# Query weight means from ScalarE sums over the transposed tiles, without the natural copy, in a new order

## The chip, the cores and the metric

The kernel runs on one core of a Trainium2 chip. The metric is the device time of one execution in microseconds (us), lower is better. TensorE is written PE, VectorE DVE, ScalarE ACT, GpSimd POOL and SyncE SP, as in the profile. SP only issues DMAs; ACT issues two of its own at the start.

## The reference

One pre-norm transformer block on 2048 tokens of width 640, in bf16: linear attention with 32 heads of size 20 and a learned softmax feature map, then a gated product without activation.

```
def _A_ref(x, wqkv, w_phi, wo):
    qkv = (x @ wqkv).reshape(B, S, 3, H, Dh).transpose(2, 0, 3, 1, 4)
    q, k, v = qkv[0], qkv[1], qkv[2]
    pq = jnp.einsum("bhsd,hdf->bhsf", q, w_phi)
    pk = jnp.einsum("bhsd,hdf->bhsf", k, w_phi)
    phi_q = jnp.concatenate([_softmax(pq), _softmax(-pq)], axis=-1)
    phi_k = jnp.concatenate([_softmax(pk), _softmax(-pk)], axis=-1)
    kv = jnp.einsum("bhsf,bhsd->bhfd", phi_k, v)
    z  = jnp.einsum("bhsf->bhf", phi_k)
    num = jnp.einsum("bhqf,bhfd->bhqd", phi_q, kv)
    den = jnp.einsum("bhqf,bhf->bhq", phi_q, z)[..., None] + 1e-6
    return (num / den).transpose(0, 2, 1, 3).reshape(B, S, D) @ wo

h  = x + _A_ref(_layernorm(x), wqkv, w_phi, wo)
h2 = h + ((_layernorm(h) @ w_gate) * (_layernorm(h) @ w_up)) @ w_down
```

## The kernel before

The tokens are 16 tiles of 128. The mean that layernorm subtracts is taken out of the weights instead of the tokens: each column of the query, key and value weights loses its mean over the 640 inputs. For queries and keys the weights are also multiplied by the feature map in advance, so that one product per token tile gives the exponents. That needs the weights transposed: `WT[:, 0, a, :]` is the a-th of five transposed tiles of the query weights (written by a DMA transpose, `wqT`), `WT[:, 1, ...]` the same of the key weights (made by PE transposes of the natural copy `Wnat`). In the profile WT and Wnat both appear under the name phiqT, whose memory they share.

The small per-head matrices w_phi are loaded as `Wrows` (25 KB) by a DMA that ACT issues; five operations, three on DVE and two on POOL, spread them into `Phi`, the block-diagonal matrix with which every transposed weight tile is multiplied (the products `x0` to `x4` for the keys, `y0` to `y4` for the queries).

The start runs as follows. PE warms up on 38 products with ones, then for each of five rows of key weights takes five one-column products with ones (the means) and five transposes; ACT and DVE copy the first two transposed groups, DVE turns the means into `nmean` (line 775) and POOL spreads these into `nmuk` (line 777, tile outb); ACT (line 803) and DVE (line 806) subtract the mean from the other groups; then PE forms x0 to x4, with the statistics of the first tokens (`s0`, `s2`) and the column sums of the value weights (`wv`) between them. After that come keys `k`, values `v`, queries `q`, the sum over tokens `A`, the attention output `n`, the output weights `h`, and the gated product `f` and `D`.

The query means (`wq_means`) come a little later: 25 one-column products of the natural query weights with ones, a copy of the result to `nmeanq` (line 820), and five operations that add `nmeanq` to the transposed tiles (lines 829 and 832).

Every operation is recorded with its reads and writes and belongs to a named unit; the table `ORDER` says, for each of the five engines, in which order the units stand. Each engine's program is emitted in exactly that order, with semaphore waits where a value comes from another engine, so an instruction that waits holds everything behind it on its engine, the DMAs that this engine issues included. Where a unit has several operations on an engine, its name stands once for each. `place()` runs a model of times that decides how buffers are shared; a DMA recorded with `at=` counts there as landed at that time, wherever its engine issues it.

Of the kernel before, what the change touches and what calls it, by code (L numbers as in the profile page):

```python
# [7 lines left out]
ACT = mybir.ActivationFunctionType  # L8
# [39 lines left out]
WQ_POOL = ()  # L48

# [48 lines left out]
    "DVE":  # L98
# [16 lines left out]
    "ACT":  # L115
# [17 lines left out]
    "POOL":  # L133
# [300 lines left out]
def _build(ctx, nc, A_x, A_wqkv, A_w_phi, A_wo, B_w_gate, B_w_up, B_w_down, out):  # L434
# [5 lines left out]
    def regs(n):  # L440
        return [Reg() for _ in range(n)]
# [1058 lines left out]
```

## Time and profile before

| | us |
|---|---|
| median of 3 runs | 267.84 (267.67 to 268.1) |
| profiled execution, its own time | 267.55 |
| span of the profile, first to last instruction | 265.8 |
| PE busy | 260.4 (98%) |
| DVE busy | 222.7 (84%) |
| POOL busy | 190.1 (72%) |
| ACT busy | 177.2 (67%) |

The profiled execution is 0.29 us under the median, and 1.75 us of it lie outside the span. Busy is time in which an engine executes; matmuls overlap each other, so a row of them lasts a little longer than the distance to the next row. In rows of the timeline the columns are start, duration, engine, line, operation, output and inputs, shape, count, and in brackets the idle time before the row with what ended it.

### The profile page before, as it was taken

To read this page: it belongs to the slowest core of one execution; us is meant where nothing else is said; L and a number is where in the kernel's file an instruction comes from. 1 tells how busy PE (TensorE), PEld (TensorE's weight loads), DVE (VectorE), ACT (ScalarE), POOL (GpSimd) and SP (SyncE) were. 2 spreads that over 40 slices of the span, in tenths; PEclk is the share of its full clock that TensorE was granted. 3 is DMA by queue.
4 is the path that set the end of the run, shared out by engine and by line. 5 is a ranking of instruction groups with operands and counts; after the bars stand their busy time and mean duration, and the time that the engine had idled before them with its cause. 6 is when DMAs were issued, how large, how long until landed. Compare 5 with 4: busy or idle time off the path is not lost.

```text
span 265.8 us, 6243 instructions
## 1 busy us (share of the span) xinstructions
PE 260.4 (98%) x2418; PEld 200.0 (75%) x2433; DVE 222.7 (84%) x417; ACT 177.2 (67%) x387; POOL 190.1 (72%) x243
## 2 busy tenths in 40 slices
PE   8999999999999999999999999999999999999995
PEld 8877777776877787777767887777777777777773
DVE  1999999999999876998999778988778788675683
ACT  2567999999857998769553695764857555645220
POOL 5446989999932889999974789359866575648652
PEclk9999999999999999999999999999999999999999
DMA  7997999903155789666856515300410401001012
GB/s 188 302 138 175 165 233 401 382 32 75 39 82 100 89 247 210 130 106 133 131 115 128 47 25 79 99 4 0 56 45 19 83 0 52 1 2 51 14 65 71
DMA packets 67390, 28.65 MB, mean 108 GB/s; under 512 B 57632, under 2 KB 66080, under 8 KB 67360
## 3 DMA queue, kind: packets, MB, share of 16 engines
q1 hardware_dynamic: 66432, 27.90, 48.7%
q10 hardware_dynamic: 928, 0.35, 0.5%
q8 instruction: 19, 0.31, 0.5%
q14 instruction: 11, 0.09, 0.1%
HBM read 11.82 MB, written 2.62 MB: 54 GB/s over the span
## 4 chain that ended last, share of the span: by engine, by line
PE 85%; DVE 5%; DMA 3%; ACT 3%; issue 1%; POOL 1%; SPq 0%; ACTq 0%
PE ps L657 60%; PE ps L1210 24%; DMA phiqT<-eq 3%; ACT eq L933 1%; DVE ob L1075 1%; PE ps L746 1%; DVE x_all L1093 1%; DVE ps L925 1%; DVE Sq L987 1%; ACT phiqT L1335 0%; POOL eq L999 0%; DVE rden L1073 0%; DVE phiqT L806 0%; ACT junk L650 0%; ACT eq L1220 0%
## 5 line engine op out<-in xcount | busy, mean ns | idle before, releaser
L657 PE MATMUL ps<-Wp,xT 128*128 128x320 bf16 (+1 forms) x606 | 89.1, 299 | 0.0
L657 PEld LDWEIGHTS ps<-Wp,xT 128*128 128x128 bf16 x606 | 58.0, 98 | 22.5 <-ACT phik L933 0.3
L1240 POOL TENSOR_TENSOR phik<-phik,gate 128x512 bf16<-128x512 bf16 x34 | 40.1, 1184 | 25.9 <-DVE phik L1237 25.5
L1220 ACT ACTIVATE eq<-ps 128x256 f32<-128x256 f32 x110 | 37.4, 386 | 23.0 <-PE ps L1210 18.6
L1210 PE MATMUL ps<-phik,Wgu 128*128 128x256 bf16 (+1 forms) x214 | 46.6, 299 | 0.2
L950 POOL TENSOR_TENSOR phik<-phik,Rk 128x1280 bf16<-128x1280 bf16 x16 | 37.4, 2357 | 5.8 <-DVE Rk L949 4.8
L657 PE MATMUL ps<-phik,Wgu 128*128 128x256 bf16 (+1 forms) x259 | 33.2, 280 | 0.1
L657 PEld LDWEIGHTS ps<-phik,Wgu 128*128 128x128 bf16 x260 | 25.0, 98 | 5.5
L1337 POOL TENSOR_TENSOR phiqT<-phiqT,x_all 128x320 f32<-128x320 f32 x26 | 21.7, 844 | 9.7 <-ACT phiqT L1335 9.6
L925 DVE TENSOR_REDUCE ps<-ps 128x1 f32<-128x640 f32 (+1 forms) x32 | 26.1, 818 | 2.8 <-PE ps L657 2.8
L1210 PEld LDWEIGHTS ps<-phik,Wgu 128*128 128x128 bf16 x228 | 21.9, 98 | 5.7 <-ACT eq L1220 0.2
L657 PE MATMUL ps<-vaug,phik 128*128 128x63 bf16 (+1 forms) x308 | 25.9, 238 | 0.0
L987 DVE TENSOR_REDUCE Sq<-eq 128x66 f32<-128x1320 bf16 x16 | 24.2, 1513 | 1.4 <-ACT eq L933 1.4
L1237 DVE TENSOR_TENSOR phik<-ps,eq 128x512 bf16<-128x512 f32 x28 | 19.1, 687 | 6.3 <-PE ps L1210 6.2
L1335 ACT ACTIVATE phiqT<-ps 128x320 f32<-128x320 f32 x26 | 11.4, 437 | 19.3 <-PE ps L657 19.2
L947 DVE TENSOR_REDUCE Ssum<-phik 128x64 f32<-128x1280 bf16 x16 | 23.3, 1460 | 0.0
L1235 DVE TENSOR_TENSOR gate<-ps,eq 128x512 bf16<-128x512 f32 x27 | 18.5, 685 | 5.2 <-PE ps L1210 2.9
L657 PEld LDWEIGHTS ps<-vaug,phik 128*128 128x128 bf16 x308 | 18.1, 97 | 5.3
L999 POOL TENSOR_TENSOR eq<-eq,rq 128x660 bf16<-128x660 bf16 x16 | 20.9, 1305 | 0.8
L933 ACT ACTIVATE eq<-ps,nb,rs 128x300 bf16<-128x300 f32 (+2 forms) x26 | 17.2, 689 | 6.1 <-DVE nb L928 4.5
L1342 DVE TENSOR_TENSOR outb<-ps,phiqT 128x320 bf16<-128x320 f32 x28 | 13.4, 487 | 6.9 <-PE ps L657 5.5
L1139 ACT ACTIVATE gate<-ps 128x256 bf16<-128x256 f32 (+1 forms) x26 | 10.4, 406 | 10.3 <-PE ps L657 9.6
(168 smaller groups left out, 526.2 us busy)
## 6 DMA issues: line engine op xcount, KB each, us to landing
x_all<-in_A_x_dram SPq DMA_DIRECT2D x4, 640.0 KB, 10.7
out_dram<-outb SPq DMA_DIRECT2D x14, 160.0 KB, 1.9
Wgu<-in_B_w_gate_dram SPq DMA_DIRECT2D x1, 1920.0 KB, 10.6
Wgu<-in_B_w_up_dram SPq DMA_DIRECT2D x1, 1920.0 KB, 16.3
vaug<-in_B_w_down_dram SPq DMA_DIRECT2D x1, 1920.0 KB, 8.5
Wp<-in_A_wqkv_dram SPq DMA_DIRECT2D x1, 800.0 KB, 5.0
phiqT<-in_A_wqkv_dram SPq DMA_DIRECT2D x1, 800.0 KB, 6.4
Wo<-in_A_wo_dram SPq DMA_DIRECT2D x1, 800.0 KB, 6.0
```

The lines of the kernel that those rows point to most:

```text
L657: ins = e.matmul(o_, lhsT=l_, rhs=r_, start=s_, stop=p_, skip_group_check=True)
L925: g.op("DVE", lambda e: e.tensor_reduce(out=mx(), in_=src(), axis=AX.XY if len(src().shape) == 3 else AX.X, op=ALU.max, apply_absolute_val ...
L933: g.op("ACT", lambda e, s=s, sc=sc, to=to, of=of: e.activation(out=to(s), in_=of(), func=ACT.Exp, bias=nb[:, i:i + 1], scale=sc[:, t:t + 1 ...
L947: g.op("DVE", lambda e: e.tensor_reduce(out=Ssum[:, vs.i, :], in_=x, axis=AX.X, op=ALU.add), rd=R_phik[t], wr=vs.R, use=[vs], t=1.39, lat=1.5)
L950: g.op("POOL", lambda e: e.tensor_tensor(out=x, in0=x, in1=Rk[:, vr.i, :].unsqueeze(2).to_broadcast([P, 2 * H, DH]), op=ALU.mult), rd=vr.R ...
L987: g.op("DVE", lambda e: e.tensor_reduce(out=Sq[:, vs.i, :].rearrange("p (w g) -> p w g", w=NQ), in_=feat(0, NQ).rearrange("p w (g f) -> p ...
L999: return e.tensor_tensor(out=x, in0=x, in1=rq[:, vr.i, :].rearrange("p (w h) -> p w h", h=HW).unsqueeze(3).to_broadcast([P, NQ, HW, DH]), ...
L1210: ins = e.matmul(o_, lhsT=l_[0](c), rhs=m_, start=fr, stop=False, skip_group_check=True)
L1220: g.op("ACT", lambda e: e.activation(out=half(s[i], 256 * h, 256 * (h + 1)), in_=PS[v.i][:, bk, 256:512], func=ACT.Copy), rd=[v.R[bk]], wr ...
L1237: g.op("DVE", lambda e: e.tensor_tensor(out=hhT[:, hb_, ft, :], in0=PS[v.i][:, 1, :], in1=half(s[1]), op=ALU.add), rd=[v.R[1]] + s[1].R, w ...
L1240: g.op(eng, lambda e: e.tensor_tensor(out=hhT[:, hb_, ft, :], in0=hhT[:, hb_, ft, :], in1=gate[:, vg.i, :], op=ALU.mult), rd=R_out + vg.R, ...
L1337: g.op("POOL", lambda e: e.tensor_tensor(out=slot(x), in0=slot(x), in1=x_all[:, t, c], op=ALU.add), rd=x.R + [R_h[t]], wr=x.R, use=[x], t= ...
```

## The change

Five ACT sums over the transposed tiles (`wm0` to `wm4`, each with an accumulated row sum) give the query means, each in a register of its own; the 25 products with ones, the copy to `nmeanq` and the load of the natural query weights (`lwq`, 800 KB) are gone. The times that the planner's model assumes for loads and transposes are changed, and `ORDER` is written anew from start to end.

```
     def wq_means():
-        U("wm")
-        v = Buf(p_ps, 2)
-        g.op("PE", lambda e: mms(e, mean_mms(PS[v.i][:, 0, :], range(NC), 0)), rd=R_Wnat + [R_one], wr=v.R, use=[v], t=0.64, lat=0.79)
-        g.op("ACT", lambda e: e.activation(out=nmeanq[:, :], in_=PS[v.i][:, 0, 0:NC], func=ACT.Copy, scale=-1.0 / SC),
-             rd=[v.R[0]], wr=[R_nmu], use=[v], t=0.1, lat=0.23)
+        for a in range(NC):
+            U("wm%d" % a)
+            act_sum(WT[:, 0, a, :], ACT.Identity, nmeanq[:, a:a + 1], [R_WT[0][a]], [R_nmu[a]], scale=-1.0 / D)
...
-    U("lwq")
-    load_wnat(0)
     for a in range(NC):
         wqT(a)
...
     "ACT":
-        "in in in wk wk wk x2 x0 x4 k0 k0 k3 wm k1 k1 v2 v3 k3 k2 wq1 k2 v5 wq3 k7 v7 k7 k4 k4 v4 k6 k6 k5 v0 k5 s12 y4 y2 s12 y0 "
+        "in wk in wk wk in x2 x0 x4 wm4 wm2 k0 k0 k3 v3 k1 k1 k3 v2 wm3 k2 k2 wm0 wq3 v7 k7 k7 wm1 v5 wq1 v4 k6 k6 k4 k4 v0 k5 k5 "
```

Three places where instructions moved. First the start of ACT. Before (L549 is a DMA issue, L612 a one-element activation, L787 the copy of a transposed key group that waits for PE, L803 and L861 as above):

```order
L549 DMA phiqT<-in_A_wqkv_dram 128x2x640
L549 DMA Wrows<-in_A_w_phi_dram 128x5x20
L612 ACT_TABLE_LOAD
L612 ACTIVATE junk<-ones 128x1
L787 ACTIVATE phiqT<-ps 128x5x128
L803 ACTIVATE phiqT<-ps,nmean 128x384 x2
L861 ACTIVATE Wp<-ps 128x640 x3
```

The same place of ACT in the changed kernel, where the lines are L547, L610, L782, L794 and L846 and the new sums are L648:

```order
L547 DMA phiqT<-in_A_wqkv_dram 128x2x640
L782 ACT_TABLE_LOAD
L782 ACTIVATE phiqT<-ps 128x5x128
L547 DMA Wrows<-in_A_w_phi_dram 128x5x20
L794 ACTIVATE phiqT<-ps,nmean 128x384 x2
L610 ACTIVATE junk<-ones 128x1
L846 ACTIVATE Wp<-ps 128x640 x3
L648 ACTIVATE junk,nmeanq<-phiqT 128x640 x2
```

The DMA for Wrows now stands behind the copy that waits for PE, and two of the new sums stand behind the evacuations of x2, x0 and x4.

Second, the start of DVE, before (L784 is the copy of the first transposed key group, L636 spreads Wrows into Phi):

```order
L784 COPY phiqT<-ps 128x5x128
L636 TENSOR_TENSOR Phi<-Wrows,G 128x140 x2
L775 TENSOR_SCALAR nmean<-ps 128x5
L636 TENSOR_TENSOR Phi<-Wrows,G 128x160
L806 TENSOR_SCALAR phiqT<-ps,nmean 128x384 x3
```

The start of DVE in the changed kernel:

```order
L779 COPY phiqT<-ps 128x5x128
L634 TENSOR_TENSOR Phi<-Wrows,G 128x140 x2
L634 TENSOR_TENSOR Phi<-Wrows,G 128x160
L770 TENSOR_SCALAR nmean<-ps 128x5
L797 TENSOR_SCALAR phiqT<-ps,nmean 128x384 x3
```

The key means moved behind all three operations that read Wrows.

Third, PE from the last key product x4 on, before (Phi,phiqT is x4, xT with itself a token statistic, Wp,xT a projection, ones,phiqT the query means):

```order
L657 MATMUL ps<-xT 128x129 x5
L657 MATMUL ps<-Phi,phiqT 128x140 x2
L657 MATMUL ps<-Phi,phiqT 128x80 x2
L657 MATMUL ps<-Phi,phiqT 128x140 x2
L657 MATMUL ps<-xT 128x129 x5
L657 MATMUL ps<-Wp,xT 128x320 x30
L657 MATMUL ps<-ones,phiqT 128x1 x25
L657 MATMUL ps<-Wp,xT 128x320 x30
```

The same place of PE in the changed kernel:

```order
L655 MATMUL ps<-Phi,phiqT 128x140 x2
L655 MATMUL ps<-Phi,phiqT 128x80 x2
L655 MATMUL ps<-Phi,phiqT 128x140 x2
L655 MATMUL ps<-xT 128x129 x10
L655 MATMUL ps<-Wp,xT 128x320 x60
```

The 25 one-column products are gone from between the projections.

On SP the load lwq goes, the transposes of the query weights and of later token tiles follow the first four token tiles at once, and the loads of the gate and up weights move from ahead of the transposes of the first query features to between them.

More of the change, by code (lines that the diff above doesn't have):

```diff
@@ L47 @@
 CEN_POOL = ()
-WQ_POOL = ()
 NB = NT // 4
@@ L537, in _build @@
     R_Wo, R_Wgu, R_Wd = regs(NC), regs(2), Reg()
-    R_wsum, R_nmean, R_nmu, R_nmuk = regs(NC), regs(NC), Reg(), Reg()
+    R_wsum, R_nmean, R_nmu, R_nmuk = regs(NC), regs(NC), regs(NC), Reg()
     R_mv, R_sm, R_sxx, R_msq = regs(NT), regs(NT), regs(NT), regs(NT)
@@ L548, in load, with transpose @@
     def load(out_, in_, wr, mb, eng="SP", at=0.0):
-        return g.op(eng, lambda e: e.dma_start(out_, in_), wr=wr, dma=("w", 8), t=0.5, lat=0.4 if at else 1.9, size=mb / 0.38, at=at)
-    def transpose(out_, in_, rd, wr, use=(), t=1.27, size=1.07, lat=0.5, at=0.0):
+        return g.op(eng, lambda e: e.dma_start(out_, in_), wr=wr, dma=("w", 8), t=0.5, lat=0.4 if at else 0.6, size=mb / 0.38, at=at)
+    def transpose(out_, in_, rd, wr, use=(), t=1.27, size=0.45, lat=0.3, at=0.0):
         return g.op("SP", lambda e: e.dma_start_transpose(out_(), in_()), rd=rd, wr=wr, use=use, dma=("tr", 8), t=t, lat=lat,
@@ L587, in load_xT @@
     def load_xT(t, at=0.0):
-        transpose(lambda: xT[:, t, :, 0:P], lambda: A_x[0, P * t:P * (t + 1), :], [], [R_xT[t]], t=1.5, size=0.75, lat=1.25 if at else 2.75, at=at)
+        transpose(lambda: xT[:, t, :, 0:P], lambda: A_x[0, P * t:P * (t + 1), :], [], [R_xT[t]], t=1.5 if at else 1.4, size=0.75 if at else 0.62, lat=1.25 if at else 2.1, at=at)
     def load_x(b):
-        load(x_all[:, 4 * b:4 * b + 4, :], A_x[0, 4 * P * b:4 * P * (b + 1), :].rearrange("(t p) n -> p t n", p=P), [R_x[b]], 1.2)
+        load(x_all[:, 4 * b:4 * b + 4, :], A_x[0, 4 * P * b:4 * P * (b + 1), :].rearrange("(t p) n -> p t n", p=P), [R_x[b]], 0.9)
     def load_wv(c0, c1, at):
@@ L686, in f @@
                 return mms(e, lst)
-            g.op("PE", f, rd=[R_xT[t], R_one, R_xone], wr=[v.R[j // 2]], use=[v], t=0.125 if act else 0.282, lat=0.275 if act else 0.43)
+            g.op("PE", f, rd=[R_xT[t], R_one, R_xone], wr=[v.R[j // 2]], use=[v], t=0.19 if act else 0.282, lat=0.34 if act else 0.43)
             if act:
@@ L719, in stats @@
                 0.22, rd=R_sm[sl], wr=R_mv[sl])
-    def mean_mms(ps, cs, c0):
-        return [(ps[:, a:a + 1], Wnat[:, c, P * a:P * (a + 1)], ones[:, 0:1], a == 0 and c == c0, False) for c in cs for a in range(NC)]
     def wk_rounds():
@@ L797, in wk_rounds @@
             n = D - P * NRAW
-            if a in WQ_POOL:
-                pool_op(lambda e, a=a: e.tensor_scalar(out=WT[:, 0, a, :], in0=WT[:, 0, a, :], scalar1=nmeanq[:, a:a + 1], scalar2=None,
-                                                       op0=ALU.add), 1.0, rd=[R_nmu, R_WT[0][a]], wr=[R_WT[0][a]])
-                continue
             if a in (1, 3):
@@ L816, in wq_means @@
     def wq_means():
-        U("wm")
-        v = Buf(p_ps, 2)
-        g.op("PE", lambda e: mms(e, mean_mms(PS[v.i][:, 0, :], range(NC), 0)), rd=R_Wnat + [R_one], wr=v.R, use=[v], t=0.64, lat=0.79)
-        g.op("ACT", lambda e: e.activation(out=nmeanq[:, :], in_=PS[v.i][:, 0, 0:NC], func=ACT.Copy, scale=-1.0 / SC),
-             rd=[v.R[0]], wr=[R_nmu], use=[v], t=0.1, lat=0.23)
+        for a in range(NC):
+            U("wm%d" % a)
+            act_sum(WT[:, 0, a, :], ACT.Identity, nmeanq[:, a:a + 1], [R_WT[0][a]], [R_nmu[a]], scale=-1.0 / D)
         for a in range(NC):
             U("wq%d" % a)
-            if a in WQ_POOL:
-                pool_op(lambda e, a=a: e.tensor_scalar(out=WT[:, 0, a, :], in0=WT[:, 0, a, :], scalar1=nmeanq[:, a:a + 1], scalar2=None,
-                                                       op0=ALU.add), 1.0, rd=[R_nmu, R_WT[0][a]], wr=[R_WT[0][a]])
-                continue
             if a in (1, 3):
                 g.op("ACT", lambda e, a=a: e.activation(out=WT[:, 0, a, :], in_=WT[:, 0, a, :], func=ACT.Identity, bias=nmeanq[:, a:a + 1]),
-                     t=0.66, lat=0.8, rd=[R_nmu, R_WT[0][a]], wr=[R_WT[0][a]])
+                     t=0.66, lat=0.8, rd=[R_nmu[a], R_WT[0][a]], wr=[R_WT[0][a]])
                 continue
             g.op("DVE", lambda e, a=a: e.tensor_scalar(out=WT[:, 0, a, :], in0=WT[:, 0, a, :], scalar1=nmeanq[:, a:a + 1], scalar2=None,
-                                                       op0=ALU.add), t=0.3, lat=0.42, rd=[R_nmu, R_WT[0][a]], wr=[R_WT[0][a]], port=True)
+                                                       op0=ALU.add), t=0.3, lat=0.42, rd=[R_nmu[a], R_WT[0][a]], wr=[R_WT[0][a]], port=True)
     def wq_round(i):
@@ L1003, in queries @@
             SLOT_USERS.append(transpose(lambda w0=w0, w1=w1: phiqT[:, bb, w0:w1, P * tt:P * (tt + 1)], lambda w0=w0, w1=w1: eq[:, b.i, P * w0:P * w1],
-                      b.R + [R_pad], [R_phiqT[bb][k][tt]], [b], t=0.254 * (w1 - w0), size=0.214 * (w1 - w0)))
+                      b.R + [R_pad], [R_phiqT[bb][k][tt]], [b], t=1.3, size=0.5, lat=0.35))
     KVBUF = Buf(p_ps, 2)
@@ L1371, in wqT @@
         U("t%d" % a)
-        transpose(lambda: WT[:, 0, a, :], lambda: A_wqkv[:, P * a:P * (a + 1)], [], [R_WT[0][a]], t=1.5, size=0.75, lat=2.75)
+        transpose(lambda: WT[:, 0, a, :], lambda: A_wqkv[:, P * a:P * (a + 1)], [], [R_WT[0][a]], t=1.4, size=0.62, lat=2.1)
     U("warm")
@@ L1385, in _build @@
     U("lwo")
-    load(Wo[:, :, 0:D], A_wo.rearrange("(c p) n -> p c n", p=P), R_Wo, 1.5)
+    load(Wo[:, :, 0:D], A_wo.rearrange("(c p) n -> p c n", p=P), R_Wo, 0.95)
     for b in range(NB):
```

132 rows, old and new, of the table ORDER are left out of this document.

## The prediction

> **What bounds the kernel now.** I read the page's busy times first, then the busy time by stretches, then the timeline of the first 18 us engine by engine, since nearly all of the edit lies there.
>
> ```profile
> PE 260.4 (98%) x2418; PEld 200.0 (75%) x2433; DVE 222.7 (84%) x417; ACT 177.2 (67%) x387; POOL 190.1 (72%) x243
> ```
> ```profile
> 10.00:20.00 10.00, 10.00 (x116) 7.83 (x114) 9.85 (x22) 6.22 (x9) 4.55 (x13) 1.00 1.15 180
> 20.00:30.00 10.00, 10.00 (x88) 7.52 (x86) 9.60 (x25) 8.65 (x12) 7.25 (x9) 1.00 0.88 180
> ...
> 60.00:80.00 20.00, 19.71 (x303) 15.46 (x302) 19.26 (x39) 15.67 (x29) 15.51 (x12) 1.00 0.39 67
> 80.00:100.00 20.00, 19.90 (x205) 16.19 (x204) 17.12 (x30) 17.82 (x43) 13.07 (x23) 1.00 0.71 149
> 100.00:150.00 50.00, 49.73 (x448) 37.44 (x448) 44.72 (x85) 31.93 (x68) 42.22 (x56) 1.00 0.75 127
> 150.00:200.00 50.00, 49.63 (x408) 38.14 (x414) 41.20 (x76) 34.75 (x97) 37.34 (x48) 1.00 0.24 44
> ```
>
> After each stretch stand its length and the busy time of PE, weight loads, DVE, ACT and POOL, then the granted clock and the DMA share. From 10 us on PE is never idle for more than tenths: over 60 to 200 us it lacks 0.29 + 0.10 + 0.27 + 0.37 = 1.03 us. So from the moment that PE runs continuously, the end is that moment plus PE's work. Work taken from PE shortens the run; time that PE loses before its steady run is not caught up, save part of that 1.03 us. DVE is as full in 10 to 30 us (19.45 of 20), so it cannot help to catch up either. The question is when the steady run begins.
>
> ```profile
> 6.15 0.85 DVE L636 TENSOR_TENSOR Phi<-Wrows,G 128x140 bf16<-128x140 bf16 x2
> 7.36 0.17 DVE L775 TENSOR_SCALAR nmean<-ps 128x5 f32<-128x5 f32 x1 [0.36 <-PE ps L657]
> 7.44 0.32 DVE L636 TENSOR_TENSOR Phi<-Wrows,G 128x160 bf16<-128x160 bf16 x1
> 7.95 1.07 DVE L806 TENSOR_SCALAR phiqT<-ps,nmean 128x384 bf16<-128x384 bf16 x3 [0.19 <-PE ps L746]
> ```
> ```profile
> 7.46 0.44 PE L746 MATMUL ps<-ident,phiqT 128*128 128x128 bf16 x5
> 7.86 0.47 PE L657 MATMUL ps<-Phi,phiqT 128*128 128x140 bf16 x6
> 8.17 0.45 PE L657 MATMUL ps<-xT 128*128 128x129 bf16 x5
> 8.45 0.48 PE L657 MATMUL ps<-Phi,outb 128*128 128x140 bf16 x6
> 9.14 0.47 PE L657 MATMUL ps<-Phi,phiqT 128*128 128x140 bf16 x6 [0.21 <-DVE sm L698]
> ```
>
> The row at 7.86 is x1, the first user of Phi; it follows DVE's last Phi operation (7.44 + 0.32 = 7.76). The row at 9.14 is x3, which follows the last of the three subtractions on DVE (7.95 + 1.07 = 9.02). The steady run begins at 9.14.
>
> **The DMA of Wrows, moved behind a waiting copy.**
>
> ```profile
> 0.78 0.46 ACTq L549 DMA_DIRECT2D phiqT<-in_A_wqkv_dram  x1
> 1.28 0.49 ACTq L549 DMA_DIRECT2D Wrows<-in_A_w_phi_dram  x1
> ...
> 6.44 0.70 ACT L787 ACTIVATE phiqT<-ps 128x640 bf16<-128x640 bf16 x1 [3.15 <-PE ps L746]
> ```
> ```profile
> phiqT<-in_A_wqkv_dram ACTq DMA_DIRECT2D x1, 320.0 KB, 3.9
> ...
> Wrows<-in_A_w_phi_dram ACTq DMA_DIRECT2D x1, 25.0 KB, 4.6
> ```
> ```profile
> 5.98 0.86 POOL L636 TENSOR_TENSOR Phi<-Wrows,G 128x140 bf16<-128x140 bf16 x2 [1.93 <-DMA Wrows<-in_A_w_phi_dram]
> ```
>
> Before, the load is issued at 1.28, lands 4.6 us later at 5.88, and POOL, which had waited 1.93 us for it, starts at 5.98. Now it stands behind the copy that PE releases at 6.44. ACT works its list in order, so the issue comes at about 6.46, 5.2 us later than before. How long it then takes no row shows under these conditions. From below: the shortest load or store of the trace, 1.7 us. From above: 6.4 us, the 800 KB load issued at 7.94. Nearest are the same load's 4.6 us, which include the passage of 320 KB issued 0.5 us ahead on the same queue, and the 3.9 us of those 320 KB, which found ACT's queue empty, as the load does now. I take 3.9: landing at 10.4.
>
> ```profile
> out_dram<-outb SPq DMA_DIRECT2D x4, 80.0 KB, 1.7
> ...
> phiqT<-in_A_wqkv_dram SPq DMA_DIRECT2D x1, 800.0 KB, 6.4
> ```
>
> From the landing on the chain is forced by DVE's new order: 0.1 to the start (5.88 to 5.98 before), two Phi operations 0.85, the third 0.32, the means 0.17 with 0.05 to the next, three subtractions 1.07, and 0.12 to PE (9.02 to 9.14), in all 2.68. So x3 starts at 10.4 + 2.68 = 13.1 instead of 9.14: **+3.9 us**. The bounds 1.7 and 6.4 give +1.7 and +6.4. Behind the waiting Phi operations on DVE stand the key means, and with them POOL's nmuk, ACT's two subtractions, and behind x1 on PE everything else: nothing can be done ahead, and no later step has 3.9 us to give back.
>
> **The clock of PE.** While PE waits it stands still from about 7.7 (its transposes and the first statistic end there) to x1 at 10.4 + 0.1 + 0.85 + 0.32 + 0.1 = 11.8.
>
> ```profile
> 0.82 4.21 PE L657 MATMUL ps<-const-bfloat16-1.0 128*128 128x128 bf16 x38 [0.82 <-PEq L1485]
> ```
> ```profile
> 262.00:265.00 3.00, 0.88 (x7) 0.39 (x4) 1.08 (x3) 0.00 (x0) 0.00 (x0) 1.00 0.33 109
> 265.00:265.80 0.80, 0.00 (x0) 0.00 (x0) 0.00 (x0) 0.00 (x0) 0.00 (x0) 0.82 0.00 0
> ```
>
> At the start 38 products of 128 columns take 4.21 us, 111 ns each; the five transposes of 128 columns at 7.46 take 0.44 us with the way through the array in it, so PE then runs at about twice that rate. At the end PE falls still at 262.9 and the granted clock of the last 0.8 us is 0.82, so it has gone down within 2.9 us of the last product. A pause of 4.1 us is longer than that. So I expect PE to run its first products after the pause at half rate. What that costs is bounded by nothing (the short products x1 and x1's second part within the wait keep it up) and by half the stretch that was slow at the start, some 5 us from 0.82 on: 2.5 us. I take 1.0, two microseconds at half rate, nearer the lower end because about 0.9 us of products (the rows of 0.3 us distance at 7.86, 8.17 and 8.45) fall inside the wait and part of the slow time passes during it. The Trainium skill says the same in "TensorE: Matmul & The Clock Gate" (Part 1, the HAM clock gate): an idle window of about 3.4 us takes PE to 1.2 GHz, and a busy one brings it back; by it the loss would be up to 1.7 us for one window, and none if the free-running window falls badly for the gate.
>
> **The products removed.**
>
> ```profile
> 16.80 0.77 PE L657 MATMUL ps<-ones,phiqT 128*128 128x1 bf16 x25
> 17.43 4.24 PE L657 MATMUL ps<-Wp,xT 128*128 128x320 bf16 x30
> ```
>
> From the start of the 25 products to the next row are 0.63 us, all in PE's steady run: **-0.63**.
>
> **The sums added.** Each is one activation of 640 columns with a read of the accumulator, as in ACT's sums over Wo and x:
>
> ```profile
> 36.23 0.74 ACT L650 ACTIVATE junk<-x_all 128x640 bf16<-128x640 bf16 x1
> 36.85 0.20 ACT L650 ACTIVATION_READ_ACCUMULATOR junk<-x_all 128x1 f32 x1
> 36.95 1.30 ACT L861 ACTIVATE Wp<-ps 128x640 bf16<-128x640 f32 x2
> ```
> ```profile
> 15.50 0.88 ACT L933 ACTIVATE phik<-ps,nb,rs 128x640 bf16<-128x640 f32 x1 [2.19 <-DVE nb L928]
> ```
>
> From row to row 36.95 - 36.23 = 0.72 us, so five take 3.6 us. Two (1.44 us) stand where ACT idled 2.19 us for the first keys. Three (2.2 us) come in the next ten microseconds, where ACT has 1.35 us left (8.65 of 10), so about 0.8 us of ACT's work slides later; the copies and exponents there free score buffers for PE. The cover is the buffers that PE still has and the 3.8 us that ACT idles in 10 to 20; if it is gone PE waits for those 0.8 us. I cost it at nothing and keep 0.8 for the range.
>
> **The load removed and the rest of the new order.** lwq's 800 KB lie in saturated DMA time (share 1.15 in 10 to 20 us), but PE names no DMA as what it waits for after 9.14, so earlier transposes gain nothing. On SP the gate and up weights now follow transposes of the first query features, on POOL the order of small operations changes; what can be won by all this is the 1.03 us above, and a loss of the same size is as possible, since PE's spare time says how closely the orders fit. I take nothing, and ±1.0 for the range.
>
> **The sum.** 267.55 + 3.9 + 1.0 - 0.63 = 271.8 in terms of the profiled execution. The median is 0.29 above that execution, so 272.1.
>
> **The rivals.**
>
> *The load comes through quickly and PE keeps its clock.* For it: 25 KB are little, and a store of 80 KB needs only 1.7 us. Against it: the DMA share is over 1 around the new issue time, and the same 25 KB needed 4.6 us. With a landing 2.6 us after issue x3 starts at 11.7, +2.6, and without the clock term the time is 267.84 + 2.6 - 0.63 = 269.8; with 3.9 us and no clock term it is 271.1. The Trainium skill gives about 2.0 us fixed for one small DMA in "DMA: Bandwidth & Descriptors" (Anatomy of one DMA, measured there for GpSimd's path); by that the sum without the clock term would be 269.2, and the 4.6 us of this trace speak against it.
>
> *ACT becomes what PE waits for.* If the sliding work meets full score buffers, or the gate weights now hold up the query features behind them on SP, PE loses 0.8 to 2 us on top: 273 to 274. For it speaks that ACT is busy 17.82 of 20 us at 80 to 100; against it, that PE waits there for 0.10 us now.
>
> *The load isn't late: faster.* If ACT's list let a DMA pass the waiting copy, Wrows would land at 5.9 as before, and only the gains would stand: 267.84 - 0.63 = 267.2, and a little less, since DVE's third Phi operation now fills the 0.36 us for which DVE waits for the means. The point from which this decides is a landing before about 6.5, when DVE's chain is no later than now. Against it: no DMA row of ACT or SP in the timeline starts ahead of the row that its program puts before it.
>
> **How the numbers follow.** Late load with a clock drop, 270.9 to 273: 0.50. Late load, quick or without the drop, 269.2 to 270.9: 0.32. ACT or SP adds more, above 273: 0.10. Absorbed to within 0.2% (0.5 us, about what a measurement can tell from no change): 0.04. Not late: 0.04. The likeliest is 272.1; the range from 269.7 to 274.0 leaves out the fastest landings below, the worst pile-up above, and the two small cases. Faster 0.03, same 0.04, slower 0.93.
>
> **What would show it.** Right: ACT issues Wrows at about 6.5; POOL and DVE wait for its landing until 9 to 11; x1 starts near 11.8 and x3 near 13.1; the 25 one-column products are absent; the first key projections have twice their spacing for about two microseconds; from then on PE idles no more than before. Wrong: Wrows issued near 1.3 or landed before 8, x3 before 11, or PE stalls after 20 us that make up more than 1 us.

## The result, and the profile after

| | before | changed |
|---|---|---|
| median, us | 267.67 (267.04 to 268.1, 5 runs) | 276.46 (275.41 to 276.55, 5 runs) |
| profiled execution, its own time | 267.55 | 275.41 |
| span | 265.8 | 273.7 |

The ratio is 1.0322, with an interval of 1.0304 to 1.0340: 8.8 us slower, where 4.3 were forecast. The profiled execution is the fastest of the five, with a mean granted clock of 0.994; the other four had 0.988 and took 276.3 to 276.55 us.

The page's first line, and PE by stretches (columns as in the prediction):

```profile
PE 262.3 (96%) x2408; PEld 200.3 (73%) x2408; DVE 224.2 (82%) x417; ACT 180.5 (66%) x396; POOL 189.8 (69%) x243
```
```profile
12.00:14.00 2.00, 1.38 (x14) 1.41 (x15) 1.63 (x6) 1.15 (x3) 0.98 (x2) 0.54 0.71 129
14.00:16.00 2.00, 2.00 (x18) 1.64 (x16) 1.77 (x5) 0.00 (x0) 0.79 (x2) 0.61 0.74 139
```
```profile
30.00:40.00 10.00, 9.53 (x76) 6.52 (x74) 9.77 (x17) 9.87 (x16) 8.57 (x8) 1.00 0.89 213
...
80.00:100.00 20.00, 19.26 (x194) 15.19 (x195) 18.30 (x38) 15.30 (x34) 8.78 (x15) 1.00 0.74 125
...
150.00:200.00 50.00, 48.72 (x414) 37.10 (x412) 40.45 (x78) 31.33 (x87) 35.97 (x47) 1.00 0.32 53
```

The start, on ACT, DVE and PE:

```profile
6.24 0.70 ACT L782 ACTIVATE phiqT<-ps 128x640 bf16<-128x640 bf16 x1 [3.67 <-PE ps L741]
6.25 0.38 ACTq L547 DMA_DIRECT2D Wrows<-in_A_w_phi_dram  x1
```
```profile
11.24 1.20 DVE L634 TENSOR_TENSOR Phi<-Wrows,G 128x140 bf16<-128x140 bf16 x3 [5.12 <-DMA Wrows<-in_A_w_phi_dram]
```
```profile
12.62 0.76 PE L655 MATMUL ps<-Phi,phiqT 128*128 128x140 bf16 x6 [4.90 <-DVE nmean L770]
...
14.31 0.81 PE L655 MATMUL ps<-Phi,phiqT 128*128 128x140 bf16 x6
...
18.52 8.31 PE L655 MATMUL ps<-Wp,xT 128*128 128x320 bf16 x60
```

The load of Wrows is issued behind the copy, as forecast, and lands 5.0 us later. x3 starts at 14.31 instead of 9.14 (+5.17), the first key projections at 18.52 instead of 12.71 (+5.81): the further 0.64 us is the half clock, which the two windows show (2 x 0.46 + 2 x 0.39 = 1.70 us lost, so 3.4 us at half rate, of which about 0.5 us fall into PE's wait). With 0.63 us of products gone, 5.2 of the 7.9 us are explained at this point. The other 2.7 us come later, and the stretches show PE idle in three places where it was not before. I follow the last of them, around 150 us; that it counts for more than the other two is not shown.

There the seven-product stage begins: for the later token blocks `fu_seven` forms the gated products from seven half-size products, and ACT keeps halves of them (line 1220 before, 1205 now; "snapshots" below) in the memory of `eq`, where the exponents of the last queries stood until their DMA transposes into `phiqT` have read them. Before, on SP (the third of these transposes is issued at 144.53), ACT and PE:

```profile
141.93 3.89 SPq L553 DMA_TRANSPOSE phiqT<-eq  x3
```
```profile
148.97 0.38 ACT L1220 ACTIVATE eq<-ps 128x256 f32<-128x256 f32 x1 [2.21 <-DMA phiqT<-eq]
```
```profile
149.13 0.38 PE L1210 MATMUL ps<-Wp,phiqT 128*128 128x256 bf16 x2
149.41 0.39 PE L1210 MATMUL ps<-phiqT 128*128 128x256 bf16 x2
```

And after, where SP issues three such transposes in a row and the last one behind an output store:

```profile
148.04 3.92 SPq L551 DMA_TRANSPOSE phiqT<-eq  x3
152.01 0.58 SPq L1279 DMA_DIRECT2D out_dram<-outb  x1
152.63 1.22 SPq L551 DMA_TRANSPOSE phiqT<-eq  x1
```
```profile
157.06 0.66 ACT L1205 ACTIVATE eq<-ps 128x256 f32<-128x256 f32 x2 [3.59 <-DMA phiqT<-eq]
```
```profile
157.50 0.39 PE L1195 MATMUL ps<-phiqT 128*128 128x256 bf16 x2 [0.67 <-ACT eq L1205]
```

Before, the first snapshot ends at 149.35 and PE goes on at 149.41, 0.06 us later than its products follow each other anyway (0.22): the last transpose arrives just in time, with no slack. After, PE waits 0.67 us for the snapshot, a quarter of the 2.7 us. From the first snapshot to the end of the execution are 267.55 - 148.97 = 118.6 us before and 275.41 - 157.06 = 118.4 after. So the whole difference of the two executions is there when the first snapshot starts. The same holds for the experiments (profiled execution of each, us):

| kernel | last transpose issued | first snapshot | own time | own time less snapshot |
|---|---|---|---|---|
| before | 144.53 | 148.97 | 267.55 | 118.6 |
| before_stores | 145.97 | 150.24 | 268.79 | 118.6 |
| after_wrows | 146.51 | 149.39 | 268.05 | 118.7 |
| after_wrows_short | 146.74 | 151.40 | 269.76 | 118.4 |
| late_mid | 147.43 | 151.33 | 269.87 | 118.5 |
| late_stores | 146.97 | 150.99 | 269.36 | 118.4 |
| late_new | 147.51 | 151.74 | 270.13 | 118.4 |
| before_sums2 | 147.43 | 152.15 | 270.69 | 118.5 |
| after_wrows_pool | 148.28 | 152.55 | 270.44 | 117.9 |
| early_new | 148.22 | 152.59 | 271.15 | 118.6 |
| after_wrows_ones | 148.66 | 152.89 | 271.24 | 118.4 |
| before_sums | 148.94 | 153.53 | 272.06 | 118.5 |
| after_wrows_sp | 150.92 | 155.56 | 273.91 | 118.4 |
| before_late | 151.93 | 156.40 | 274.96 | 118.6 |
| after | 152.63 | 157.06 | 275.41 | 118.4 |
| after_warm | 154.49 | 157.38 | 275.83 | 118.5 |
| after_again | 155.62 | 159.88 | 278.23 | 118.4 |

The last column says where the time is lost, ahead of the snapshot, but not that the snapshot is the cause. Nearly the same work of PE stands behind the snapshot in every kernel, so the column would come out the same wherever ahead of it the time was lost; late_stores below is such a case.

### The profile page after: what moved, and what is told of

It reads as the page before. It is cut to its first block, busy times and chain, and to the rows that moved or that the text cites. A ratio compares the mean times of both kernels' runs of the same rounds, so it can differ in the third digit from the quotient of the medians.

```text
span 273.7 us, 6222 instructions
## 1 busy us (share of the span) xinstructions
PE 262.3 (96%) x2408; PEld 200.3 (73%) x2408; DVE 224.2 (82%) x417; ACT 180.5 (66%) x396; POOL 189.8 (69%) x243
## 4 chain that ended last, share of the span: by engine, by line
PE 70%; DMA 7%; POOL 6%; DVE 6%; ACT 5%; SPq 3%; issue 2%; ACTq 0%; DVEq 0%
PE ps L655 48%; PE ps L1195 22%; DMA phiqT<-eq 4%; SPq L551 3%; ACT eq L918 2%; DMA Wrows<-in_A_w_phi_dram 2%; POOL phik L935 2%; DVE Sq L972 1%; DMA phik<-ob 1%; POOL eq L984 1%; DVE phik L1133 1%; ACT junk L648 1%; POOL Wp L1149 1%; POOL rs L1098 1%; DVE ob L1060 1%
## 5 line engine op out<-in xcount | busy, mean ns | idle before, releaser
L1205 ACT ACTIVATE eq<-ps 128x256 f32<-128x256 f32 x112 | 38.2, 386 | 25.6 <-PE ps L1195 21.1
L1195 PE MATMUL ps<-phik,Wgu 128*128 128x256 bf16 (+1 forms) x228 | 51.0, 305 | 0.6 <-ACT t L1205 0.6
L655 PE MATMUL ps<-phik,Wgu 128*128 128x256 bf16 (+1 forms) x260 | 33.9, 281 | 0.1
L1220 DVE TENSOR_TENSOR gate<-ps,eq 128x512 bf16<-128x512 f32 x29 | 19.8, 686 | 7.8 <-PE ps L1195 3.1
L1222 DVE TENSOR_TENSOR phik<-ps,eq 128x512 bf16<-128x512 f32 x27 | 18.5, 686 | 5.9 <-PE ps L1195 5.9
L655 PE MATMUL ps<-Phi,phiqT 128*128 128x63 bf16 (+3 forms) x236 | 13.3, 203 | 6.1 <-DVE nmean L770 4.9
```

Of the source, the lines that this page charges most:

```text
L655: ins = e.matmul(o_, lhsT=l_, rhs=r_, start=s_, stop=p_, skip_group_check=True)
L1195: ins = e.matmul(o_, lhsT=l_[0](c), rhs=m_, start=fr, stop=False, skip_group_check=True)
L1205: g.op("ACT", lambda e: e.activation(out=half(s[i], 256 * h, 256 * (h + 1)), in_=PS[v.i][:, bk, 256:512], func=ACT.Copy), rd=[v.R[bk]], wr ...
L1220: g.op("DVE", lambda e: e.tensor_tensor(out=gate[:, vg.i, :], in0=PS[v.i][:, 0, :], in1=half(s[0]), op=ALU.add), rd=[v.R[0]] + s[0].R, wr= ...
```

## The experiments: the start

Ratios are to the kernel before, run on the same chip, with 95% intervals. In diffs of the order, the name ahead is the engine.

**after_wrows.** The late load undone.

```
ACT
- in wk in wk wk in x2 x0 x4 wm4
+ in in in wk wk wk x2 x0 x4 wm4
```

> The changed kernel with one thing undone: ScalarE again issues the load of Wrows before its first copy, as in the kernel before; the sums and the rest of the new order stay. Theory A (the loss has two parts: the late Wrows, which starts the first key projection 5.8 us later, 5.2 us of it wait and 0.6 us clock, and another 2 to 3 us of stalls further on that the sums or the new order make): 276.5 - 5.2 - 0.6 to 1.7 = 269.6 to 270.7 us, still slower than before, and the stall of TensorE near 35 to 37 us (about 1 us) is there 5 to 6 us earlier. Theory B (everything follows from the late Wrows): 267.7 - 0.6 = 267.0 us. The wait of VectorE for Wrows (5.12 us) is gone in both.

Median 270.47 us (268.05 to 271.69), ratio 1.0111 (1.0093 to 1.0130). Six us of the loss are the late load, 2.7 are not: theory A. The profiled execution is the fastest of its seven runs (five took 270.35 to 270.49), so its trace is not typical of the 2.7 us.

**before_late.** The late load alone, the opposite edit to the kernel before.

> The kernel before with one thing changed: ScalarE issues the load of Wrows behind its first copy, in the changed kernel's place; no sums, old order otherwise. Theory A (the late Wrows costs the same by itself): 267.7 + 5.2 + 0.6 to 1.7 = 273.5 to 274.6 us, Wrows landing near 11.2 us and a stretch of half clock between 10 and 16 us. Theory C (the load is slow in the changed kernel only because other loads were reordered around it): landing 3.9 us after its issue, as forecast, and 272 to 273 us. Theory D (the start is mostly absorbed later): under 271 us.

Median 273.88 us, ratio 1.0236 (1.0212 to 1.0259): 6.1 us, the same from the other side, so theory C and D fall. The landing was later than in the changed kernel's profile. The chain of waits (start, duration, what):

```profile
6.42 6.42 DMA Wrows<-in_A_w_phi_dram
```

**after_again.** The changed kernel a second time.

> The changed kernel unchanged, for a second profile of it: the first one was of its fastest execution (275.4 us, clock 0.994), while its other four took 276.3 to 276.6 us at a clock of 0.988. Theory A (in those, Wrows lands later than the 5.0 us of the first profile, by up to 1.5 us, and a second stretch of half clock falls into the start): landing near 6.4 us, half clock for 6.8 us. Theory B (the landing is the same, and the difference lies in the later stages): landing near 5.0 us.

Its profiled execution took 278.23 us (clock 0.988), 1.7 us more than the slowest of the first five; the other one took 275.76. Chain, PE and clock:

```profile
6.04 6.99 DMA Wrows<-in_A_w_phi_dram
```
```profile
14.43 0.76 PE L655 MATMUL ps<-Phi,phiqT 128*128 128x140 bf16 x6 [6.92 <-DVE nmean L770]
...
20.85 3.42 PE L655 MATMUL ps<-Wp,xT 128*128 128x320 bf16 x24
```
```profile
10.00:12.00 2.00, 0.00 (x0) 0.00 (x0) 0.00 (x0) 0.00 (x0) 0.00 (x0) 0.90 0.61 87
12.00:14.00 2.00, 0.00 (x0) 0.00 (x0) 0.95 (x3) 0.00 (x0) 0.90 (x2) 0.50 1.08 192
14.00:16.00 2.00, 1.57 (x16) 1.60 (x17) 1.62 (x7) 1.15 (x3) 0.79 (x2) 0.50 0.71 138
16.00:18.00 2.00, 2.00 (x15) 1.49 (x13) 1.76 (x5) 0.00 (x0) 0.79 (x2) 0.50 1.75 108
18.00:20.00 2.00, 2.00 (x27) 1.67 (x26) 1.01 (x4) 0.56 (x1) 1.44 (x5) 0.89 0.38 81
```

Theory A: the same load in the same place lands 5.0 us after its issue in one execution and 7.0 in another, and with the longer pause comes a second stretch of half clock (3.42 us of clock missing in these windows, 6.8 us at half rate; the part up to 14.43 falls into the pause itself).

**after_warm.** PE kept busy while it waits.

```
+        U("w2")
+        g.op("PE", lambda e: mms(e, [(PS[vx[1].i][:, 0, 0:P], one, one, True, True) for _ in range(80)]), ...
PE
- wk wk s0 x1 s0 x1 x3
+ wk wk s0 w2 x1 s0 x1 x3
```

> The changed kernel with 80 products of a 128-column constant put on TensorE between its first statistics and the first product that waits for Phi; they do no work for the result and end before the wait does (80 x 0.056 us = 4.5 us of the 4.9 us). Theory A (the wait costs a stretch of half clock as well as itself): the clock stays at 1.0 up to the end, and the time falls by the 0.6 us seen in the profiled execution up to the 1.7 us of one whole window, to 274.8 to 275.9 us. Theory B (the clock is no part of the loss): 276.5 us, or more if the products hold the first waiting product back.

Median 276.38 us (275.71 to 277.28), no different from 276.46: in the time, theory B. But the profile shows the clock kept up and the landing late:

```profile
6.32 6.56 DMA Wrows<-in_A_w_phi_dram
```
```profile
14.29 0.47 PE L655 MATMUL ps<-Phi,phiqT 128*128 128x140 bf16 x6 [1.80 <-DVE nmean L770]
...
19.08 5.19 PE L655 MATMUL ps<-Wp,xT 128*128 128x320 bf16 x37
```

From x1 to the first key projections are 19.08 - 14.29 = 4.79 us here, 18.52 - 12.62 = 5.90 with one stretch of half clock and 20.85 - 14.43 = 6.42 with two; before it was 12.71 - 7.86 = 4.85. So the clock costs 1.1 to 1.6 us at the start. That the medians don't show it I can't settle: the landing varies by more (1.6 us between these two profiles), and only profiled executions show it.

## The experiments: the sums and the new order

All kernels of this section have Wrows early.

**after_wrows_short.** The sums' time taken away.

```
- act_sum(WT[:, 0, a, :], ..., scale=-1.0 / D)
+ act_sum(WT[:, 0, a, 0:32], ..., scale=-1.0 / 32)
```

> The changed kernel with the early Wrows, and each of the five ScalarE sums taken over 32 of the 640 columns: order, waits and dependences stay, only the time of the sums falls, by about 5 x 0.5 us (the means are then rough ones). Theory A (ScalarE is the crowded engine between 13 and 41 us, and the sums' own time is what is left of the loss): 270.5 falls by 2 to 3.4 us, to 267 to 268.5 us. Theory B (the rest of the loss is the new order, not the sums): unchanged within 0.5 us, 270 to 271 us.

270.30 us, ratio 1.0106 (1.0090 to 1.0121): unchanged. In this order the sums' own time costs nothing that can be measured.

**after_wrows_ones.** The new order without the sums.

```
- act_sum units wm0 to wm4, R_nmu of five registers
+ U("lwq"); load_wnat(0); U("wm") with the 25 products and the copy
PE:  + wm behind k3 k1     SP: + lwq ahead of t4
DVE: - k3 wq2 k3 k1 k1 wq4     + k3 k3 wq2 k1 k1 wq4
```

> The changed kernel's order with the early Wrows, and without the sums: the natural query weights are loaded again, the 25 one-column products and one copy stand where the kernel before had them among the keys, and VectorE takes wq2 one step later. It is the new order alone against the kernel before. Theory A (the sums make what is left of the loss): 267.7 us, within 0.7. Theory B (the order makes it): 270 to 271.5 us, with TensorE's stalls between 80 and 170 us as in the changed kernel.

270.53 us, ratio 1.0109 (1.0090 to 1.0128). The new order alone costs as much as order and sums together: theory B. That the products with ones cost nothing against the sums does not follow, since the 800 KB load came back with them, and PE now waits 0.52 us at 36.45 us for a transposed token tile. late_new below is the cleaner test.

**after_wrows_sp.** SP back to the old order, the other engines not.

> The changed kernel with the early Wrows and, on SyncE alone, the order of the kernel before (less the load of the natural query weights); the sums and all other orders stay. Theory A (the sums on ScalarE): unchanged, 270.5 us or a little less, since two transposed query tiles come earlier. Theory B (SyncE's new order, which issues the query features' transposes elsewhere among its loads, makes the stalls between 80 and 170 us): 268 to 269.5 us.

273.22 us, ratio 1.0214 (1.0192 to 1.0236): worse, which neither theory had. The engines' orders fit each other, and exchanging one of them alone does not tell what it is worth.

**before_sums** and **before_sums2.** The sums in the old order.

```
ACT, before_sums
- x4 k0 k0 k3 wm k1 k1 v2 v3 k3 k2 wq1 k2 v5 wq3 k7 v7 k7
+ x4 wm4 k0 k0 k3 wm2 k1 k1 v2 v3 k3 wm3 k2 wq3 k2 v5 wm1 wq1 k7 v7 wm0 k7
ACT, before_sums2
+ x4 wm4 wm2 k0 k0 k3 k1 k1 v2 wm3 v3 k3 k2 wm1 k2 wq1 v5 wq3 k7 v7 k7 wm0
```

> The kernel before with the sums alone: the 25 one-column products and the load of the natural query weights are gone, the five ScalarE sums stand where ScalarE waited in the kernel before (behind x4, behind the first exponents of k3, and between k3 and k7), Wrows stays early, all other orders as before but for wq0, which VectorE takes two key tiles later. Theory A (ScalarE has room: it is idle 4.7 us between 13 and 41 us in the kernel before, and five sums of 0.67 us less the copy of 0.17 us need 3.2 us): 267.7 - 0.6 = 267.0 us. Theory B (the sums crowd ScalarE in that stage wherever they stand, and cost what stays unexplained in the changed kernel): 269 to 270 us.

271.55 us, ratio 1.0145 (1.0128 to 1.0162). PE waits for an exponent that stands behind a sum, and DVE for the last sum:

```profile
20.80 1.53 PE L657 MATMUL ps<-Wp,xT 128*128 128x320 bf16 x10 [0.68 <-ACT phik L931]
```
```profile
31.39 1.05 DVE L830 TENSOR_SCALAR phiqT<-phiqT,nmeanq 128x640 bf16<-128x640 bf16 x1 [1.44 <-ACT junk L650]
```

> The kernel before with the sums alone, placed better than in the first such kernel: two of them in ScalarE's wait of 2.2 us ahead of the first key exponents, one in its wait ahead of v3, the last two among the exponents of k2 and k7; VectorE takes wq0 three steps later, and SyncE issues the second transposed query tile right behind the first. Theory A (the sums take the place of the 25 products at no cost if nothing waits for them): 267.0 us (-0.6), up to no change, and the 3.8 us of the first such kernel was the places: ScalarE's sums of 0.7 us on the chain ahead of exponents and evictions, and VectorE's wait of 1.4 us for the last sum. Theory B (the sums cost ScalarE's room in any place): 268.5 to 271 us.

270.85 us, ratio 1.0113 (1.0093 to 1.0134): better placed by 0.7 us, still 3.05 us slower. PE loses more than half of it in the key stage, by stretches:

```profile
20.00:30.00 10.00, 8.87 (x76) 6.60 (x77) 8.84 (x22) 9.49 (x15) 6.40 (x8) 1.00 0.85 168
30.00:40.00 10.00, 9.45 (x99) 7.13 (x97) 9.63 (x24) 8.94 (x15) 8.14 (x8) 1.00 0.83 228
```

Here the sums do cost: PE idles 1.13 + 0.55 us in these stretches; before, by the row below and the one in the prediction, 0.06.

```profile
30.00:40.00 10.00, 9.94 (x110) 7.77 (x109) 9.97 (x24) 9.52 (x16) 8.95 (x10) 1.00 0.87 206
```

I found no place for them in the old order that doesn't; that there is none isn't shown.

**early_new** and **late_new.** Orders spliced on all engines at the end of the first attention products, near 75 us: the sums and the new order ahead of it and the old order behind, and the other way round without the sums.

> The changed kernel with the early Wrows, its sums and its new order up to the end of the first attention products (near 75 us), and from there on, on every engine, the order of the kernel before. Theory A (the rest of the loss, 2.7 us, lies in the new order of the later stages, where GpSimd stands 4 us before a sum and TensorE then waits twice for its weight sums): 267 to 268 us. Theory B (it lies in the new order of the key stage, where the first query product waits for the last sums): 269.5 to 270.5 us.

269.26 us, ratio 1.0055 (1.0035 to 1.0074), runs spread from 267.57 to 271.15. The profile is of the slowest run. It is on time up to the splice and beyond: an operation on DVE that starts at 85.44 us before starts at 85.44 here. The loss comes behind that, where both kernels have the same order. SP issues two transposes right behind the load of the down weights (w_down, 1920 KB), and they take 2.6 us longer; ACT waits 2.32 us for them, and PE for ACT. Before, on SP and PE:

```profile
94.10 5.76 SPq L553 DMA_TRANSPOSE phiqT<-eq  x2
```
```profile
105.25 0.51 PE L657 MATMUL ps<-Phi,phiqT 128*128 128x63 bf16 x11 [0.22 <-ACT eq L933]
```

In early_new:

```profile
93.60 8.35 SPq L548 DMA_TRANSPOSE phiqT<-eq  x2
```
```profile
107.33 0.51 PE L652 MATMUL ps<-Phi,phiqT 128*128 128x63 bf16 x11 [1.70 <-ACT eq L915]
```

Whether the early order brings such slow transposes about, or chance does, is not shown.

> The kernel before (products with ones, natural weights loaded, its own order) up to the end of the first attention products, and from there on, on every engine, the changed kernel's order. Theory A (the late part of the order makes the loss): 269.5 to 270.5 us, with TensorE's two stalls of 0.5 to 0.8 us near 162 and 171 us that follow GpSimd's wait. Theory B (the early part makes it): 267.3 to 268.2 us.

270.44 us, ratio 1.0102 (1.0080 to 1.0124). The late part alone has the whole loss. Nothing but `ORDER` differs from the kernel before here, so neither the sums nor the planner's changed times are needed for it. The early part alone has about half of the loss in the median, and the two don't add up (1.75 + 2.93 against 2.73 with both); why is not shown.

**after_wrows_pool.** GpSimd's weight sums ahead of its wait.

```
POOL
- T3 h8 h8 h11 h10 h9 G2.1 h8 h11 G2.3 T2 f1.1.0
+ T3 h8 h8 G2.1 G2.3 T2 h11 h10 h9 h8 h11 f1.1.0
```

> The changed kernel with the early Wrows and one more edit, on GpSimd alone: three sums of weights (G2.1, G2.3 and T2) stand ahead of the statistics of tile 11, for which GpSimd waited 4.0 us with the sums behind it. Theory A (this wait delays the weight sums, and TensorE's stalls near 162 and 171 us, 0.5 and 0.8 us, are its price): 269.0 to 269.5 us, those stalls gone. Theory B (TensorE would wait for something else there): 270.5 us.

270.56 us, ratio 1.0106 (1.0076 to 1.0136): theory B by the time. GpSimd's wait comes after the first snapshot and, without this edit, for a statistic of ACT that stands behind it, so it is late because that stage is late. In the profile the edit did part of what theory A says: after_wrows_short, with the same order but for this edit (and with shorter sums), has GpSimd waiting 4.00 us up to 152.95 us and PE 0.62 up to 161.45, and here both waits are gone. From the first snapshot to the end are 117.9 us, 0.5 to 0.8 less than in all other profiles. The interval of the ratio is too wide to show half a microsecond.

**late_mid.** The new order only from 75 us to the first product of the second block's feed-forward stage.

> The kernel before up to the end of the first attention products, the changed kernel's order from there to the first product of the second block's feed-forward stage, and the order of the kernel before again from there on. Theory A (the loss of the late order lies in the stage from 75 to 150 us, where transposes, projections and feed-forward products of one block are interleaved): 269.5 to 270.5 us, as with the whole late order. Theory B (it lies in the order of the seven-product stage from 150 us on): 267.3 to 268.2 us.

269.90 us, ratio 1.0086 (1.0066 to 1.0106): theory A for the greater part (2.1 of 2.9 us; the two intervals overlap, so that the rest lies in the later order is not shown). Most of the time is lost ahead of the seven-product stage, in when it can begin.

**before_stores.** The last transpose delayed, and nothing else.

```
SP
- Q15 n14 Q13 Q13 Q15 n12 ... h9 h10 d0 d1 D0.1
+ Q15 n14 Q13 Q13 d0 d1 Q15 n12 ... h9 h10 D0.1
```

> The kernel before with one edit on SyncE: the two stores of the first output tiles, which it issues some 10 us later otherwise, stand ahead of the last transpose of the query features (Q15's), which is issued at 144.53 us in the kernel before and for whose landing ScalarE waits 2.2 us with its first snapshot for the seven-product stage at 148.97 us. A store takes 0.58 us of issue. Theory A (the last query-feature transpose sets the start of the seven-product stage, so that whatever makes it later makes the end later by as much): last transpose and first snapshot 1.2 us later, time 268.5 to 269.0 us. Theory B (that stage has slack, and the kernels' losses lie elsewhere): 267.5 to 267.9 us.

268.50 us, ratio 1.0032 (1.0021 to 1.0044); the profiled execution 268.79, 1.24 us above that of before, its first snapshot 1.27 us later. SP, ACT and PE:

```profile
144.87 1.05 SPq L1294 DMA_DIRECT2D out_dram<-outb  x2
145.97 1.22 SPq L553 DMA_TRANSPOSE phiqT<-eq  x1
```
```profile
150.24 0.38 ACT L1220 ACTIVATE eq<-ps 128x256 f32<-128x256 f32 x1 [3.23 <-DMA phiqT<-eq]
```
```profile
149.39 0.38 PE L1210 MATMUL ps<-Wp,phiqT 128*128 128x256 bf16 x2
150.68 0.39 PE L1210 MATMUL ps<-phiqT 128*128 128x256 bf16 x2 [0.91 <-DVE phiqT L1164]
```

Theory A: the last transpose was the cause here. The operations of ACT and DVE stand in the same order in both kernels; just ahead of the snapshot they start 0.25 us later than before, and from 157 us to the end 1.27 us later. Two stores of half a microsecond of issue on SP thus cost the run 0.9 us in the median. (The row names a DVE operation that ends at the same moment as the snapshot; before, the same product at 149.41 starts ahead of that operation, which stands at 149.61, so it isn't what the product needs.)

**late_stores.** The store that the new order puts ahead of the last transpose, behind it.

```
SP
- Q15 Q15 Q13 d1 Q13 n12
+ Q15 Q15 Q13 Q13 d1 n12
```

> The kernel before with the changed kernel's order after the first attention products, and with one edit on SyncE: the store of an output tile, which there stands ahead of the last transpose of the query features, stands behind it. Theory A: last transpose and first snapshot 0.6 us earlier (147.5 and 151.7 us without the edit), time 269.8 us instead of 270.4. Theory B: 270.4 us, unchanged.

Last transpose 0.54 us earlier, first snapshot 0.75, the profiled execution 0.77 (269.36 against 270.13). But the two profiles differ ahead of the edit too, by up to 1.3 us in the same order (a sum on DVE starts at 122.11 instead of 120.80). The median of 270.02 is 0.4 us lower than that of late_new, while the ratio of 1.0110 (1.0071 to 1.0149), which one run of 273.27 raises, is higher than its 1.0102: the interval holds both theories.

The profile shows something else. PE doesn't wait for the snapshot at 150.99 any more: the chain that ended last runs on PE alone from 140 to 156 us.

```profile
139.93 9.92 PE ps L655 x80
149.85 0.44 PE ps L1208 x4
150.29 1.92 PE ps L655 x15
152.21 1.31 PE ps L1208 x11
```

Still this execution takes 1.8 us more than that of the kernel before. So the late transposes are one place at which the late order costs time (PE waits 0.58 us for the first snapshot in late_new's profile, 0.67 in the changed kernel's), and not all of it: here most of the time is lost ahead of 140 us, at steps that no run singles out.

None of these kernels beats the kernel before.

## Why the prediction was wrong

The step that failed is the price of the new order, nothing within 1.0 us: it costs 2.9 us. The late load was right in kind and 1.1 us too cheap, and no run shows the 0.63 us that the removed products were to give back. Without the first of these the other two would leave 272.1 + 1.1 + 0.6 = 273.8, inside the range.

- *Late Wrows, mechanism:* right. Issue at 6.25 (6.46 forecast), DVE waits, PE stands still, x1 is late. By itself it cost 6.0 us (after_wrows) and 6.1 (before_late) where load and clock were forecast at 4.9.
- *Its landing, 3.9 us:* mis-sized. It measured 4.97, 6.42, 6.56 and 6.99 in four profiles, the last two beyond the upper bound of 6.4. The row taken, 3.9 us for 320 KB issued at 0.78 on an empty queue, was near by queue and far by the load on the DMA engines (in the changed kernel their share is 1.18 from issue to landing of Wrows, while it was 0.94 in the kernel before); that this is the reason is not shown. The upper bound was no bound.
- *The chain from the landing to x3, 2.68 us:* 14.31 - 11.22 = 3.09, since the products ahead of x3 ran at half clock (0.54 to 0.60 us from row to row instead of 0.3). With the landing this makes +5.17 for +3.9.
- *The clock, +1.0:* 1.1 to 1.6 us between x1 and the first key projection (0.4 of it already counted in the 5.17), so the size was about right, but how many stretches a pause costs differed between two executions.
- *The products removed, -0.63:* gone from PE, and no run shows a gain: after_wrows_ones has them, with the load, and takes the same time. What failed beneath it is "the end is that moment plus PE's work". It holds only while PE's work alone sets the moments behind it.
- *The sums at nothing:* right in the new order (after_wrows_short), wrong for the old one (3 to 4 us in two placements).
- *The new order at 0 +-1.0:* this is the term that put the time outside the range. It measured +3.0 (after_wrows_ones) and +2.9 (late_new), 2.1 of it in the order between 75 and 150 us (late_mid). The step took PE's 1.03 us of idle time for the size of what can be lost, but that time only bounds what can be won. And "PE names no DMA as what it waits for after 9.14" was taken from waits of PE itself. Two places of the profile before say otherwise. One is on ACT: a snapshot that waits 2.21 us for a DMA and lets PE go on 0.06 us later; in before_stores a delay there passes to the end. The other is in the chain that ended last: PE leaves it at 74.11 us and takes it up again at 105.25, and between stand DVE, POOL, ACT and a transpose.

```profile
94.10 8.54 DMA phiqT<-eq
...
105.25 31.85 PE ps L657 x305
```

In PE's own waits such a chain shows here only as tenths (0.22 us at 105.25).
- *The rivals:* "ACT or SP adds more", at 0.10, came nearest, since it named SP's transposes of the query features. Neither of its reasons is what the runs show: late_new has no sums and leaves the loads of the gate and up weights where they were, and has the whole loss. Its price of 0.8 to 2 us was also too low.
- What stays open: why the same load lands 5.0 us after its issue once and 7.0 another time, why most executions of after_wrows take 2.4 us more than its profiled one, and which of the moved steps between 75 and 145 us (the load of the down weights is one) make the last transposes 3.0 us later in late_new, and the run longer even where PE doesn't wait for them.

## What to carry to other kernels

Before costing a reorder at nothing, look for waits that end just in time: on every engine, the work that was released late (here 2.2 us of waiting on ACT) and whose user then starts at once. A DMA put behind a compute instruction in an engine's program costs that instruction's wait and also its own landing at that moment, which need not be the one it had at another (here 4.6 us issued at 1.28, 5.0 to 7.0 issued at 6.0 to 6.4). And splicing two orders at a stage boundary on all engines tells which part of a reorder brings a loss, while exchanging one engine's order does not; where the time goes has still to be read from the trace, and it can lie behind the splice.

## What the hardware showed that was not expected

- A load of 25 KB took 5.0 to 7.0 us from issue to landing with a DMA share of 1.1 to 1.3 meanwhile, and its time varied by 2 us between executions of one program. The Trainium skill's figure for one small DMA, about 2.0 us ("DMA: Bandwidth & Descriptors", Anatomy of one DMA, given there for GpSimd's path), was not met by any late load here.
- The half clock came in stretches of 3.4 us, one for a pause of PE of 4.9 us and two for one of 6.9 us, and so the same program paid 1.1 us in one execution and 1.6 in another. This agrees with "TensorE: Matmul & The Clock Gate" of the Trainium skill (Part 1, the HAM clock gate), which calls the window of about 3.4 us free-running and what is slow at its start variable by run.
- The last transpose of `eq` needed 3.9 to 4.7 us from its issue to the snapshot that it releases in 15 of the profiles and 2.9 us in two (after_wrows and after_warm), where the median landing of such transposes in this stretch of the kernel before is 2.7:

```profile
phiqT<-eq SPq DMA_TRANSPOSE x4, 2.7
```

After_wrows's profile is of the fastest of its seven executions, after_warm's of the second fastest of its five.
